# A hand-written order of steps for a delta-rule attention and a folded feed-forward: the same steps listed in another order

## The chip, the cores and the metric

One core of a Trainium2 chip runs the kernel. The metric is the device time of one execution in microseconds (us). Five engines work in parallel, each through its own instructions in the order in which they stand: TensorE (PE; its weight loads are shown as PEld), VectorE (DVE), ScalarE (ACT), GpSimd (POOL) and SyncE (SP), which here only issues DMA transfers. Engines wait for each other through semaphores.

## The reference

Two blocks, one after the other. The first is a recurrence over 768 tokens for 4 batches and 8 heads of size 48; the second is a feed-forward without a nonlinearity, in which two projections are multiplied element by element.

```python
k_n = k / (norm(k) + 1e-6)
for t in range(S):
    y[t]  = q[t] @ state
    v_old = k_n[t] @ state
    state = state + beta[t] * outer(k_n[t], v[t] - v_old)
x = y as (3072 tokens, 384)
a = x @ w1          # 384 x 1024
b = x @ w2          # 384 x 1024
h = (a * b) @ w3    # 1024 x 1024
out = h @ w_out     # 1024 x 384
```

The four weight matrices come as 64-bit floats, the rest as 32-bit floats.

## The kernel before, in words

The tokens are cut into 12 chunks of 64 per batch. Inside a chunk the recurrence is written as a triangular system: scores of keys against keys (`scores`, L357), the inverse of a unit triangular matrix (`inverse` L420 for 32 x 32 blocks of two chunks at a time, `corner` L476 for the off-diagonal blocks), and then products with the state (`chain` L543) and the outputs (`outputs` L619). The feed-forward starts from a product of weights: since no nonlinearity stands between w3 and w_out, the kernel first computes w3 @ w_out once (`fold` L756), which needs all of w_out and, transposed on TensorE, all of w3. After that each pair of chunks u (512 tokens) needs a = x @ w1, b = x @ w2, their product, and one product with the folded weights; that last one is done with seven half-size products instead of eight (`slab_sums` L835, `o` L851, `result` L901).

The kernel is written as generators. Each step has a name, a letter with a number, and each time its name comes up in the string `ORDER` (L39) it is resumed up to its next `yield`. What it issues goes to the ends of its engines' queues, and `in_text_order` (L159) fixes that order on every engine. So `ORDER` is the schedule, and nothing else decides it. The names:

- `beta`, `k0`..`k11`, `q0`, `q1`, `v0`..: loads of tokens. `p2`..: loads of k and q in another layout into one buffer each (`kperm`, `qperm`), `d2`..: their transposes on VectorE (L324). `K0`, `K1`, `Q0`, `Q1`: transposes of the first two chunks on TensorE (L337).
- `g0`..`g5` (`squares` L264) and `N0`..`N5` (`norms` L276): norms of k for two chunks, many small VectorE instructions, with one small product on TensorE each. `n0`..: v times the norm, on POOL.
- `s0`..`s11`: scores. `u0`..: their diagonal blocks stored to DRAM. `V0`..`V5`: the inverse of two chunks: V0.1 loads the blocks, two ScalarE copies bring V into PSUM (V0 and V1 only), 31 elimination steps of two VectorE instructions each follow (L440, L445), two ScalarE copies back (L449), one store (L453). `e0`..`e11`: loads of that result (L462, L469), then the corner with two products on TensorE (L498).
- `c0`..`c11`: the state chain (L551 and the VectorE lines after it). `y0`..: outputs of the chunk, copied into xT on ScalarE, and a few copies inside xT by DMA (L684).
- `P0`..`P35`: weight pieces (`piece` L695). Each is one load on SP (L699; four for w1 and w2), two ScalarE instructions (L707, L708), two VectorE instructions (L710, L711) and one POOL instruction (L715), which turn 64-bit floats into 32-bit ones. P0 to P7 are w_out, P8 to P23 are w3, P24 to P29 are w1, P30 to P35 are w2. w_out lies in the room of w2 until the folds are done. The raw data of all pieces go through five buffers in turn.
- `t0`..`t15`: transposes of the w3 pieces P8 to P23, four on TensorE and one ScalarE copy (L753). `f0`..`f7`: the folds; f7.0 needs the first half of w_out and t14, f7.1 the second half and t15, and f7.2 copies the result (L766).
- `b0`..`b7`: the a and b products of chunk 0, `a00`..`a07` those of chunk 1, `a10`.. to `a57` those of the later pairs (`ab` L772): .0 is x @ w1, .1 a ScalarE copy, .2 x @ w2, .3 the product on VectorE (L795), after which the bank is free.
- `T`: differences of the folded weights. `S0`..`S5`: sums of the products (POOL). `o0`..`o5`: the last products (L874). `x0`..`x5`: results and stores.

TensorE's results go to PSUM: four banks in turn (`bank` L149) and two double banks in turn (`two_banks` L146). A product that takes the bank of four products earlier waits until that one has been read. The transposed w3 pieces, the w3 pieces and the products a * b share ten buffers in turn (`slab` L692).

The loop that follows the string:

```python
def step(name):
    if name not in running:
        running[name] = parts[name]()
    next(running[name], None)

for name in ORDER.split():
    step(name)
in_text_order()
```

Of the kernel before, what the change touches and what calls it, by code (L numbers as in the profile page):

```python
# [36 lines left out]


ORDER = """  # L39
beta k0 P0 g0 P13 P10 P0 k1 P18 beta K0 P0 P0 P12 P13 P13 q0 P10 P18 P10 P10 K0 K0 P13 K0 beta  # L40
K0 g0 g0 q1 P8 P1 P18 g0 P12 P18 P12 K1 g0 k2 K1 K1 K1 g0 g0 P12 Q0 K1 Q0 Q0 g0 Q0 g0 P5 g0 N0
Q0 Q1 P8 P8 s0 t5 Q1 Q1 g1 Q1 Q1 s1 g1 s0 P8 g1 P9 s0 s1 s1 s1 s0 t4 t2 s0 p2 P1 P5 s0 s0 s1 s1
V0 P11 P5 P5 N0 P3 t5 P1 P1 d2 u0 P9 d2 u1 P11 P3 P9 P4 P11 N0 P3 t4 P4 P4 P9 P11 t3 t2 P2 P7
P2 P14 t0 P7 P3 P2 V0 V0 t10 P6 s1 P2 P14 t3 V0 P7 V0 V0 V0 P6 f1 g1 p3 P4 P7 t0 P14 P6 P6 P16
V0 V0 P15 V0 V0 V0 f2 V0 t10 P16 P16 f2 P15 f1 V0 f1 P16 P19 V0 V0 p2 t1 V0 P19 P19 V0 V0 f2 f0
P14 t6 t1 f0 f0 V0 P15 V0 P19 V0 v0 P15 t6 s1 P20 d2 V0 P17 P20 P20 t11 V0 P17 t11 d2 V0 t8 t8
P20 V0 k3 g1 g1 V0 g1 f5 P17 t7 V0 P17 V0 P22 P22 f5 V0 t7 V0 f5 v1 n0 V0 f3 V0 V0 s0 f3 P23
P26 V0 g1 f4 d3 t9 V0 t9 V0 d3 f4 P22 P22 f3 t14 P23 P23 P24 P24 P26 p3 t14 d3 f4 P23 n0 P30
P24 P24 s2 V0 p4 e0 g1 g1 t15 t12 f7 t15 f7 t12 f6 P26 P26 N1 e0 e0 s2 s2 P21 d3 e0 P30 e0 e0
s2 f7 s2 P25 e1 s2 c0 P21 e1 e1 e1 c0 n1 s3 P21 P21 N1 s3 y0 y0 P31 N1 s3 s3 s3 P25 P25 s3 n1  # L50
P31 c0 c0 P25 V1 P30 u2 t13 u3 P32 P30 V1 t13 e1 e1 c1 P31 V1 f6 f6 c1 c1 c1 y1 y0 b1 P32 P32
P32 y1 V1 V1 V1 b0 V1 P31 V1 b0 b2 V1 V1 b1 V1 V1 P27 P27 b1 V1 P27 V1 b1 b2 P29 P29 V1 b3 b3
P29 y1 b3 a03 V1 P28 V1 b3 P27 a01 a02 c1 a03 V1 a00 V1 k4 V1 P29 P28 P28 a01 a00 V1 V1 a00 P28
a02 a05 a00 V1 b5 V1 a05 b6 V1 V1 V1 V1 P35 p4 P35 b6 P33 a07 V1 V1 V1 V1 V1 V1 g2 a07 a04 b5
a04 b7 P33 k5 a06 b4 b7 v2 n2 a01 V1 P35 P33 a06 P34 a03 c1 V1 a03 V1 b2 V1 P35 P33 g2 P34 P34
P34 e2 b2 a01 c2 d4 d4 g2 p5 b4 b0 a04 d4 g2 g2 b0 g2 g2 e2 a07 a06 g2 g2 a04 d4 e2 n2 c2 a07
V2 b4 a06 e2 e2 e2 b5 c2 g2 N2 s4 c2 b4 S0 s4 s4 a02 a02 c2 c2 p5 T b5 T y2 b6 y2 d5 T b7 d5 d5
e3 e3 d5 N2 s4 s4 s4 N2 b7 e3 e3 v3 a05 T u4 a05 s5 b6 S0 s5 s5 S0 s5 s5 n3 o0 x0 e3 e3 s5 c3
n3 c3 S0 u5 S0 S0 S0 S0 o0 S0 S0 S0 S0 c3 c3 o0 V2 y3 x0 o0 V2 S0 V2 S0 V2 V2 V2 o0 V2 y3 V2 k6
x0 S0 g3 c3 g3 g3 S0 g3 V2 v4 x0 o0 V2 V2 V2 y3 V2 a10 a10 x0 x0 k7 x0 o0 V2 x0 x0 a17 V2 V2 V2  # L60
V2 x0 V2 V2 V2 a17 V2 V2 a15 V2 V2 a13 a16 V2 V2 v5 V2 a13 p6 V2 a16 V2 a15 V2 g3 V2 a13 g3 a13
p6 x0 a14 c3 a14 V2 e4 d6 a10 a17 a12 e4 e4 e4 g3 g3 c4 a17 g3 d6 a10 a14 d6 a12 n4 n4 c4 e4 g3
e4 e5 n5 a12 c4 a11 d6 N3 a14 c4 c4 n5 a11 y4 p7 p7 c4 e5 s6 a11 s6 s6 y4 a15 a12 a11 c5 e5 V3
a16 d7 d7 d7 d7 o1 c5 v6 a16 k8 g4 g4 e5 g4 p8 a15 g4 s7 s7 S1 e5 s7 S1 e5 x1 s7 s7 S1 s7 c5 o1
s6 S1 u7 c5 o1 s6 s6 u6 S1 S1 V3 S1 y5 c5 c5 V3 V3 V3 V3 V3 o1 S1 x1 k9 S1 y5 S1 y5 o1 S1 S1 x1
x1 V3 S1 S1 V3 c6 V3 S1 S1 V3 d8 o1 x1 x1 v7 a20 n6 x1 V3 a20 o1 x1 a23 V3 V3 x1 V3 x1 n7 a27
a24 d8 a26 V3 V3 V3 V3 x1 g4 V3 a23 V3 a25 V3 a27 a27 V3 a24 V3 V3 a26 a20 V3 g4 V3 p8 V3 V3 V3
V3 p9 V3 V3 a25 d8 n6 d8 g4 a20 a22 a22 a24 V3 c6 a27 a25 a24 a21 a21 e6 e6 e6 g4 e7 N3 e6 a25
N3 g4 s8 g4 N4 s8 e6 a22 s8 a26 e6 c6 c6 N4 s8 a26 s8 y6 a22 V4 p9 N4 S2 d9 e7 s8 a21 e7 y6 u8
d9 a21 e7 c6 a23 d9 p10 e7 d9 S2 c6 S2 s9 n7 a23 s9 e7 o2 s9 c7 s9 S2 s9 k10 S2 c7 x2 o2 c7 S2  # L70
S2 o2 u9 s9 V4 c7 V4 S2 y7 V4 V4 x2 V4 g5 g5 V4 p10 d10 y7 S2 x2 S2 o2 y7 V4 o2 x2 c7 V4 V4 S2
S2 V4 o2 a35 x2 x2 k11 x2 S2 V4 x2 S2 a35 v8 V4 S2 V4 V4 S2 V4 x2 n8 o2 a37 x2 V4 v9 V4 V4 V4
x2 a34 n8 V4 V4 a36 a30 V4 V4 V4 V4 V4 a37 V4 a34 a33 V4 g5 a33 a30 a32 a36 V4 V4 V4 V4 a34 a33
V4 V5 a32 e8 n9 c7 e8 a30 c8 a33 e8 e9 e8 g5 a35 a34 c8 a30 e8 g5 d10 a32 e9 g5 a32 g5 a36 e8
e9 S3 c8 a36 a35 a31 d10 d10 e9 a31 n9 c8 g5 c8 c8 g5 g5 e9 a31 s10 N5 e9 p11 s10 s10 a31 c9
a37 a37 p11 c9 y8 N5 v11 d11 S3 d11 d11 o3 v10 d11 s10 y8 s10 S3 u10 S3 s11 N5 s11 o3 s10 c9
s11 c9 s11 S3 x3 S3 s11 o3 S3 S3 y9 o3 s11 x3 S3 o3 u11 V5 S3 S3 V5 y9 V5 x3 n11 S3 x3 V5 V5 V5
S3 y9 S3 S3 V5 c9 V5 o3 x3 V5 x3 x3 V5 V5 x3 S3 a47 o3 x3 V5 V5 a47 x3 V5 V5 a47 n10 V5 a46 a40
a40 V5 a47 V5 a43 V5 a46 x3 a42 a45 V5 a42 V5 a41 a45 a43 V5 V5 V5 V5 V5 V5 a44 V5 a44 V5 a45
a41 V5 V5 V5 V5 c9 a42 e10 a40 e10 n11 a42 e10 a44 e10 c10 a45 n10 e11 e10 e11 c10 a43 e10 c10  # L80
c10 a40 e11 a41 a46 e11 c10 a44 S4 a43 e11 a41 S4 c10 o4 e11 a46 c11 x4 S4 S4 y10 o4 c11 c11 S4
y10 S4 S4 S4 S4 S4 c11 o4 y11 o4 x4 S4 S4 S4 o4 y11 x4 x4 o4 S4 x4 x4 S4 y11 S4 x4 x4 a50 x4 o4
a50 x4 a55 a56 a55 a52 a55 a50 a52 a56 a54 a57 a54 a55 a54 a50 a54 a51 a52 a57 a51 a53 x4 a52
a53 a51 a56 a56 a53 a51 a53 a57 o5 S5 a57 S5 S5 o5 S5 S5 S5 x5 S5 S5 S5 o5 o5 x5 S5 S5 S5 o5 S5
S5 S5 o5 x5 S5 x5 o5 x5 x5 x5 x5 x5 x5 x5 x5 x5 x5
"""


# [956 lines left out]
```

## Time and profile before

| what | value |
|---|---|
| time, median of 3 runs | 609.24 us (608.55 to 610.59) |
| profiled execution, first to last instruction | 607.4 us |
| mean granted TensorE clock | 0.966 |
| instructions | 19078 |
| PE busy | 550.0 us |
| DVE busy | 364.9 us |
| POOL busy | 177.2 us |
| ACT busy | 158.9 us |
| HBM read, written | 43.88 MB, 11.01 MB |

The profiled execution is one execution, seen from its first to its last instruction, 607.4 us; what a run needs before and after that is not in it. The page splits it into 40 slices of 15.2 us, and gives for each slice the busy share of every engine in tenths, the clock that TensorE was granted and the share of the DMA engines. Other views give the busy time of each engine in any stretch, the instructions of an engine in order of time, and whose work ended a wait. In a line such as `90.69 0.58 ACT L753 COPY w3T<-ps_f ... [5.13 <-PE ps_f L750]` the first number is the start, the second the length, then engine, line, operation and what it writes from what; in brackets stands how long the engine had been idle and what ended that.

### The profile page before, as it was taken

Reading aid. Unit: us, or ns where it says so; the run is one execution under the profiler, and the core shown is the slowest. Engines: PE = TensorE matmul, PEld = TensorE weight load, DVE = VectorE, ACT = ScalarE, POOL = GpSimd, SP = SyncE. Lnnn points to the kernel's source line nnn. Section 1 sums busy time; section 2 is a strip of 40 time slices with the busy share of each in tenths; the row PEclk is TensorE's granted clock in tenths of the full one; section 3 lists DMA queues with packets and bytes.
Section 4 is the critical chain, followed back from the end, with each engine's and each line's share of the span. In section 5 each row is a group of like instructions: output and inputs, shape, how many; then the busy total and the mean of one; then the engine's idle time right before and its main releaser. Section 6 shows DMA issues by size and latency. Waiting matters only on the chain.

```text
span 607.4 us, 19078 instructions
## 1 busy us (share of the span) xinstructions
PE 550.0 (91%) x8188; PEld 383.1 (63%) x8188; DVE 364.9 (60%) x828; ACT 158.9 (26%) x333; POOL 177.2 (29%) x223
## 2 busy tenths in 40 slices
PE   2648789678898999999999989999999999999997
PEld 2545455657777885456964559745588545984477
DVE  3768977466998489765489463894764843311012
ACT  3645534445323111222111221121112012321100
POOL 6554443122255530304420016013053000600041
PEclk9988979669999999999999999999999999999999
DMA  9968998554956347462443534435323040010001
GB/s 192 244 155 226 186 189 173 97 133 94 165 104 88 82 92 120 92 98 39 101 101 73 81 52 87 97 70 103 58 51 84 31 85 5 5 52 13 1 0 52
DMA packets 219507, 57.31 MB, mean 94 GB/s; under 512 B 206656, under 2 KB 212800, under 8 KB 219424
## 3 DMA queue, kind: packets, MB, share of 16 engines
q1 hardware_dynamic: 215232, 55.31, 45.3%
q10 hardware_dynamic: 4192, 0.79, 0.9%
q8 instruction: 64, 1.05, 0.8%
q14 instruction: 19, 0.16, 0.1%
HBM read 43.88 MB, written 11.01 MB: 90 GB/s over the span
## 4 chain that ended last, share of the span: by engine, by line
PE 75%; DVE 8%; DMA 5%; issue 4%; ACT 3%; SPq 3%; ACTq 0%; DVEq 0%
PE ps_f L779 37%; PE ps_f L874 16%; PE ps_w L551 5%; PE ps_f L759 4%; PE ps_w L652 4%; DMA raw<-in_moe_w_dram 3%; PE ps_w L498 3%; PE ps_w L367 2%; DVE tb L440 2%; PE ps_w L373 2%; SPq L230 2%; DVE ps_w L445 2%; DMA ktok<-in_k_dram 1%; ACT xT L673 1%; PE ps_f L750 1%
## 5 line engine op out<-in xcount | busy, mean ns | idle before, releaser
L779 PE MATMUL ps_f<-xT,w2s 128*128 128x512 f32 (+1 forms) x336 | 133.7, 544 | 1.6 <-issue 1.5
L779 PE MATMUL ps_f<-xT,w1s 128*128 128x512 f32 (+1 forms) x336 | 128.7, 533 | 4.5 <-DVE ab L795 2.0
L846 POOL TENSOR_TENSOR ab<-ab 128x256 f32<-128x256 f32 x96 | 67.2, 729 | 195.0 <-DVE ab L795 171.0
L779 PEld LDWEIGHTS ps_f<-xT,w1s 128*128 128x128 f32 x336 | 63.0, 190 | 60.3 <-issue 52.0
L779 PEld LDWEIGHTS ps_f<-xT,w2s 128*128 128x128 f32 x336 | 63.2, 193 | 56.2 <-issue 52.3
L791 ACT COPY ab<-ps_f 128x512 f32<-128x512 f32 (+1 forms) x56 | 28.4, 525 | 172.7 <-PE ps_f L779 161.4
L874 PE MATMUL ps_f<-w,ab 128*128 128x192 f32 x376 | 66.5, 330 | 0.0
L874 PEld LDWEIGHTS ps_f<-w,ab 128*128 128x128 f32 x376 | 61.1, 190 | 4.4 <-issue 3.5
L795 DVE TENSOR_TENSOR ab<-ab,ps_f 128x512 f32<-128x512 f32 (+1 forms) x56 | 33.2, 605 | 49.1 <-PE ps_f L779 49.0
L440 DVE TENSOR_TENSOR tb<-Vb,Ub 128x31 f32<-128x31 f32 (+15 forms) x124 | 46.0, 371 | 15.5 <-DMA Ub<-Ud 12.1
L759 PE MATMUL ps_f<-w2s,w3T 128*128 128x384 f32 x128 | 48.4, 535 | 5.7 <-ACT w3T L753 5.0
L445 DVE TENSOR_TENSOR Vb<-Vb,tb 128x31 f32<-128x31 f32 (+15 forms) x124 | 47.2, 381 | 4.3
L874 PE MATMUL ps_f<-room,ab 128*128 128x192 f32 x272 | 47.9, 330 | 1.1 <-DVE room L905 1.1
L874 PEld LDWEIGHTS ps_f<-room,ab 128*128 128x128 f32 x272 | 44.1, 190 | 1.9 <-issue 1.5
L673 ACT COPY xT<-ps_w 48x256 f32<-48x256 f32 x96 | 30.4, 365 | 48.1 <-PE ps_w L652 47.5
L759 PEld LDWEIGHTS ps_f<-w2s,w3T 128*128 128x128 f32 x128 | 26.2, 211 | 24.2 <-ACT w3T L753 5.5
L270 POOL TENSOR_TENSOR sq<-ktok 128x384 f32<-128x384 f32 x24 | 20.9, 875 | 61.4 <-DMA ktok<-in_k_dram 30.1
L367 PE MATMUL ps_w<-KQ 48*64 48x128 f32 x384 | 31.3, 308 | 3.9 <-issue 2.0
L379 DVE TENSOR_TENSOR U<-ps_w,wt 128x512 f32<-128x512 f32 x24 | 16.6, 690 | 29.9 <-PE ps_w L373 28.6
L715 POOL TENSOR_TENSOR w<-w,raw 128x512 uint32<-128x512 uint32 x16 | 20.7, 1299 | 43.6 <-DVE w L711 18.6
L373 PE MATMUL ps_w<-KQ 48*64 48x64 f32 x768 | 32.1, 242 | 0.3 <-issue 0.3
L537 POOL TENSOR_TENSOR vtok<-vtok,n 128x384 f32<-128x384 f32 x24 | 20.1, 851 | 41.0 <-DMA vtok<-in_v_dram 26.8
(109 smaller groups left out, 676.4 us busy)
## 6 DMA issues: line engine op xcount, KB each, us to landing
raw<-in_moe_w_dram SPq DMA_DIRECT2D x16, 512.0 KB, 6.2
vtok<-in_v_dram SPq DMA_DIRECT2D x24, 192.0 KB, 4.3
raw<-in_moe_w_dram SPq DMA_DIRECT2D x24, 192.0 KB, 4.0
out_dram<-osb SPq DMA_DIRECT2D x46, 96.0 KB, 2.2
ktok<-in_k_dram SPq DMA_DIRECT2D x44, 96.0 KB, 3.9
raw<-in_moe_w_out_dram SPq DMA_DIRECT2D x8, 384.0 KB, 4.8
Ud<-U SPq DMA_DIRECT2D x48, 64.0 KB, 2.1
Ub<-Ud SPq DMA_DIRECT2D x6, 512.0 KB, 3.4
```

The source lines that it names most:

```text
L367: pe.matmul(ps[half(z), 0, n : n + 128], lhsT=x[:, 0, :], rhs=x.rearrange("p j t -> p (j t)"), start=True, stop=True,)
L373: pe.matmul(ps[half(z ^ j), 1, n + C * j : n + C * j + C], lhsT=x[:, 0, :], rhs=x[:, j, :], start=True, stop=True,)
L440: dve.tensor_tensor(out=tv, in0=V[:, 0 : s + 1, s : s + 1].to_broadcast([P, s + 1, n]), in1=U[:, s, s + 1 : BS].unsqueeze(1).to_broadcast( ...
L445: dve.tensor_tensor(out=o, in0=o, in1=tv, op=ALU.subtract)
L551: pe.matmul(out(ps, r, h, z), lhsT=lhs(r, h, z), rhs=rhs(r, h, z), start=True, stop=True,)
L673: act.copy(out=xT[f, p:NP:2, b : b + NR, cc, :].rearrange("p a r t -> p r a t"), in_=pyv[f, z, b : b + NR],)
L759: pe.matmul(ps[:, 0:DM], lhsT=w3Ts[jc, kc // 4][:, kc % 4 * P : kc % 4 * P + P], rhs=wo[:, kc], start=(kc == 0), stop=(kc == KF - 1),)
L779: pe.matmul(ps[:].rearrange("p b c t -> p b (c t)"), lhsT=w[:, m, js], rhs=x[:, m, :, c0:c1].rearrange("p b c t -> p b (c t)"), start=(m = ...
L791: act.copy(out=t, in_=ps)
L795: dve.tensor_tensor(out=t, in0=t, in1=ps, op=ALU.mult)
L846: pool.tensor_tensor(out=o_, in0=x_, in1=y_, op=op)
L874: pe.matmul(ps[b][:, b, :], lhsT=abs_[u, HF * f + i][:, t0 : t0 + P], rhs=ws_[w][:, i], start=first and i == 0 and (b == 0 or n == "F"), s ...
```

## The change

The string `ORDER` is replaced by another one with the same 1317 names, each as often as before. No function is touched. All five engines get the same instructions in a different order, from the first load to the last products; the tail (o5, x5) is as before. Some places of the new string:

- SP's first loads were beta, P0, P13, P10, k1, P18; they are P10, k1, q1, P8, beta, P18. ScalarE's own queue issues q0 ahead of k0.
- w_out's eight pieces stood among P8 to P14 and P18; in the new string P5 and P2 come early and P1, P7, P6, P0, P3, P4 follow one another after P13.
- p4's first half stood between the store of V0 and the loads of e0 on SP, and now stands behind k4. v0 stood ahead of V0's store and now stands behind it. P24 and P30 stood ahead of e0 and now stand behind u2.
- f7 stood between f4 and f6 ahead of e0's first product; f7.0 now stands between e0's two products, f7.1 behind c0's second product. f6.1 stays between c1's first and second.
- In the later pairs, the a products come in another order, the w2 product of an index often directly after its w1 product.

```diff
 ORDER = """
-beta k0 P0 g0 P13 P10 P0 k1 P18 beta K0 P0 P0 P12 P13 P13 q0 P10 P18 P10 P10 K0 K0 P13 K0 beta
-K0 g0 g0 q1 P8 P1 P18 g0 P12 P18 P12 K1 g0 k2 K1 K1 K1 g0 g0 P12 Q0 K1 Q0 Q0 g0 Q0 g0 P5 g0 N0
...
-P26 V0 g1 f4 d3 t9 V0 t9 V0 d3 f4 P22 P22 f3 t14 P23 P23 P24 P24 P26 p3 t14 d3 f4 P23 n0 P30
-P24 P24 s2 V0 p4 e0 g1 g1 t15 t12 f7 t15 f7 t12 f6 P26 P26 N1 e0 e0 s2 s2 P21 d3 e0 P30 e0 e0
-s2 f7 s2 P25 e1 s2 c0 P21 e1 e1 e1 c0 n1 s3 P21 P21 N1 s3 y0 y0 P31 N1 s3 s3 s3 P25 P25 s3 n1
...
+P10 q0 Q0 k0 K0 g0 g0 g0 g0 K0 V0 K0 Q0 Q0 K0 P10 k1 g0 g0 P10 Q0 Q0 q1 Q1 P10 g0 g0 P8 K0 P8 Q1
+Q1 Q1 P8 P8 Q1 beta P18 beta beta P5 P5 g0 g0 P5 P5 K1 K1 P18 K1 P18 P18 P2 P2 P2 P2 N0 s0 t0 K1
...
+P22 P21 g1 t12 V0 t9 t8 f4 g1 P23 P23 g1 g1 P23 t9 P22 g1 g1 N1 f4 f4 t14 t14 t15 t15 v0 n0 n0
+f6 P26 N1 e0 e0 e0 s2 s2 d3 P26 e0 d3 P21 s1 N1 d3 f7 P31 P26 e0 e0 s2 P31 e1 c0 s2 t13 s2 c0 s0
+P25 y0 y0 P25 V1 c0 P26 P31 f7 u2 d3 e1 e1 e1 c0 s3 s3 s3 s3 s3 s3 P24 P28 P31 c1 c1 P24 P24 P24
...
```

## The prediction

> **What bounds the kernel now.** I read the page's engine totals and 40 slices first, then the same figures by stretch, then who TensorE waited for, then two queues in order of time where the waits pointed. Step names (s0, V0, f7.1) are those of the section on the kernel; "f7.1" is the second resumption of f7, "P24.3" the fourth of P24, counted from .0.
>
> Parts 1 and 2 of the page:
>
> ```profile
> PE 550.0 (91%) x8188; PEld 383.1 (63%) x8188; DVE 364.9 (60%) x828; ACT 158.9 (26%) x333; POOL 177.2 (29%) x223
> ...
> PE   2648789678898999999999989999999999999997
> ...
> PEclk9988979669999999999999999999999999999999
> DMA  9968998554956347462443534435323040010001
> ```
>
> TensorE is the bound, but only from the tenth slice on. Before that it starves, its clock dips, and the DMA engines are nearly full. By stretch (columns: busy of PE, PEld, DVE, ACT, POOL, then clock, DMA share, GB/s):
>
> ```profile
> 0.00:139.00 139.00, 98.11 (x1557) 70.93 (x1561) 93.09 (x202) 65.51 (x122) 59.39 (x68) 0.86 0.81 178
> 105.00:139.00 34.00, 24.79 (x859) 20.26 (x861) 17.63 (x29) 15.21 (x30) 6.66 (x7) 0.70 0.59 130
> 139.00:232.00 93.00, 86.20 (x1492) 73.36 (x1483) 73.15 (x179) 27.59 (x66) 37.40 (x44) 0.98 0.54 103
> 232.00:604.00 372.00, 365.71 (x5156) 238.85 (x5155) 198.69 (x448) 65.84 (x145) 80.39 (x112) 1.00 0.33 61
> ```
>
> At 139 us y1 ends and the first dense product (b1) begins. Idle TensorE time is 139.0 - 98.1 = 40.9 us before that, 6.8 us up to 232, 6.3 us up to 604. So an order can win much only ahead of 139 and lose much only after it. What TensorE waited for ahead of 139 (total, times, longest):
>
> ```profile
> PE ps_f L750 <- POOL w L715: 9.3, 2, 9.0
> PE ps_f L759 <- ACT w3T L753: 5.0, 2, 4.3
> ```
>
> These are weight pieces that came late. The other delay is in the chain inversion -> corner -> state, on two in-order queues, ScalarE's and SP's:
>
> ```profile
> 84.97 0.58 ACT L449 COPY Vb<-ps_w 128x512 f32<-128x512 f32 x1 [2.03 <-DVE ps_w L445]
> 90.69 0.58 ACT L753 COPY w3T<-ps_f 128x512 f32<-128x512 f32 x1 [5.13 <-PE ps_f L750]
> 91.17 0.59 ACT L449 COPY Vb<-ps_w 128x512 f32<-128x512 f32 x1
> ```
>
> ```profile
> 91.78 0.35 SPq L453 DMA_DIRECT2D Vd<-Vb  x1
> 92.23 5.46 SPq L230 DMA_DIRECT2D kperm<-in_k_dram  x8
> 97.73 0.49 SPq L462 DMA_DIRECT2D TT<-Vd  x1
> ```
>
> V0's last elimination ends on VectorE at 84.9. Its second copy then stands on ScalarE behind t9's copy, whose transposes are behind two fold halves on TensorE: 5.13 us. Then p4's eight transfers (5.46 us) stand on SP between V0's store and e0's loads.
>
> **The change part by part.** Every step is still there, so engine work, bytes and matmuls are equal; only waits can change. The sum goes against the profiled execution, span 607.4; the median of the runs shown is 609.24, 1.8 us more (start and end of the program outside the span), so a change of the span is a change of the time.
>
> *Start up to V0's eliminations.* The raw buffers (five) still pace the pieces. In the new order VectorE has P10, P8, P5, P18, P2 ahead of N0; P2 is the eighth load on SP. Loads so far, with q0 and k0 on ScalarE's queue: 3.9 MB; at the 218 to 234 GB/s of the first 30 us P2 lands near 21, its ScalarE and VectorE steps (1.0 and 0.9) end near 25, N0 begins there as before (25.0), s0's first scaling is near 30 (30.5 before), s1's last 37.6 (38.0), u1's stores leave at 38 to 40 (40.0 to 42.0). V0's load left at 47.4, behind P7 and P14; now it is behind P0 and P3, whose buffers come free near 41: 42 to 43. VectorE must still do P3 before V0; that is near 50, against 52.7. Gain 2.7; bounds -3 and +6.
>
> *V0 on VectorE.* Between first and last elimination VectorE did 31.4 us of work in 32.2. The new order leaves P6, P20, P17 and two of g1's reductions outside and takes P4 in: 28.8 us of work, 29.5 with the same gaps. End near 79.5, gain 5.4.
>
> *From V0 to e0.* t9 no longer stands ahead of the copies; f5's result (f5.1 must end, near 77), P20, P17 and P21 do, 1.2 us each on ScalarE: the second copy ends near 82.5, against 91.8. On SP p4 has gone far back, behind k4. Behind p3's q half, P23, the store, v0 and P26, e0's loads leave near 86 (97.7). v0 now follows V0's store: n0 on POOL needs it before c0, and P21's, P26's and P31's POOL parts queue behind n0; it lands near 86, c0 is due at 100, so I cost it at nothing. If that cover goes, each us is paid at t13.
> The next thing late is the norm N1: VectorE has P20, P17, P22, P21, P23 ahead of it (5.5 us), and g1's sums need TensorE behind f4.0. From V0's end the folds run without a gap (halves of 2.74, from 51.5 on): f4.0 ends near 88, N1 (4.5) near 93, f6.0 95, e0's first product near 96, against 105.3. Gain 9.3, and this replaces the gains above, which lie beside it.
>
> *e0 to y1, with f7 spread into it.* This took 34.0 us (105.3 to 139.3), with TensorE gaps of 5.5 (1.2, 0.5, 0.9, 0.7, 0.35, 0.75, 1.2). Now f7.0 and f7.1 (2.75 each at full clock, 97.4 to 102.8 before) are inside; f6.1 was already. If no gap takes them: 39.5. If they fill the gaps and the clock holds, I get 27: e0 0.8, f7.0 2.75, e0.4, s2.3, c0, y0, c0.2 with the copies between them up to 12, f7.1, s3, c1, e1, f6.1, c1.2, y1 another 12. I take 33, the middle, as the clock was reduced in part of the nearest rows:
>
> ```profile
> 110.00:120.00 10.00, 8.11 (x267) 7.44 (x267) 4.69 (x10) 2.53 (x5) 2.07 (x2) 0.51 0.45 92
> 120.00:130.00 10.00, 6.60 (x244) 5.74 (x244) 7.92 (x11) 7.27 (x16) 3.68 (x4) 0.66 0.53 120
> ```
>
> y1 ends at 96 + 33 = 129: 10.3 us earlier. Here the clock is open. The rows show 0.51 although TensorE was busy 8.1 of 10 us and no wait listed there is over 2.1 us.
>
> [...]
>
> *b and a products of the first pair, to 232.* The same 93.6 us of TensorE groups. b0.2 now comes third, so w2's first pieces are due earlier, and P24, P28, P30, P32 now stand on SP behind u2 (they were loaded at 80 to 92 and 125). From s2's last scaling: u2 3.0, P24 1.5, P28 1.7, y0's six copies 4.6, P30 1.7, u3 1.8, P32 1.8, landing 5.9 (as P32 before), then ScalarE 1.4, VectorE 1.1, POOL 2.6: about 27, so 129 for a scaling at 102; b0.2 is due at 132. Covered by 3 us; if y1 ended at 123 that cover is gone and 3 us are paid. The other moved loads (k4 and k5 swapped, v1 to v3, p4) go where DMA share is 0.54 and below; they matter only on SP: P35, k5, P34, P33, v2, k4, p4 and v3 now stand ahead of V1's store, 24 us of issue from the end of y1's copies near 136, so through at 160, and V1's last copy is due near 164. I take 0 (2 us of bank waits against the 2.0 that TensorE waited for a product's evacuation near 150); bounds -2 and +4.
>
> *From 232 on.* Two placements are tighter. After V2's first step x0.7 comes 17.4 us of VectorE work later (16.2 before), and a12 needs the bank it frees 17.3 us after c3's second product ends: 1.2 us of stall. From s5's last matmul to e4's first TensorE has 47.5 us of work; the chain through u5, V2 and e4 took 53.5 there, but 48.1 and 47.6 in the fifth and sixth pair: 2 us. a31 behind x2.9: 1. Together 4, against single stalls of 0.9, 0.2, 1.5, 0.7 and 0.8 now: 0; bounds -2 and +8. The last stores follow o5 as before: 0.
>
> Sum: -10.3 + 0 + 0. Span 597.1, time 599.
>
> **The rivals.**
> *The chain goes slower (other side).* Between e0 and y1 the clock falls to half and stays, and f7.0, f7.1, f6.1 stand in the chain at half clock. f5.1 took 5.43 so: 16.3 for three, in place of f6.1's 4.4: 34.0 - 4.4 + 16.3 = 45.9, y1 at 141.9, 2.6 late: 612. It decides from 43.3 us in this stretch. For it: 0.51 and 0.66 in just these steps. Against: the fold halves at 82 to 105 all took 2.74.
> *The clock holds.* y1 ends at 123; b0.2 then waits 3 for w2: -13.3, time 596. For it: the clock is 1.00 later, where the same small products lie between dense ones.
> *The later stages give back more.* If V2's and V5's chains take 53.5 again, against 47.5 and 47.9 of cover: 11.6 of stall in place of my 2 and 0, at worst no gain; half of that, 605. For it: 53.5 was measured. Against: 47.6 was too.
> *Nothing that counts.* A list of the same work can land within 0.3% (1.8 us, about what can be told from no change).
>
> **How the numbers follow.** Forecast 0.47 (594 to 604), clock holds 0.13, half given back 0.12: faster 0.72. Within 0.3% 0.05. Slower 0.23. The likeliest is 599. The range runs from 591 (clock holds, start 5 better) to 613 (slower chain); the likeliest one's own is 594 to 604.
>
> **What would show it.** Right: V0's last elimination near 80, its store near 83, e0's loads near 86, e0's first product near 96, y1's end near 129, then the same slope to the end, idle TensorE under 33 us ahead of b1. Wrong: e0's product after 100; a stretch over 43 us with the clock near 0.5; idle over 10 us after 232, at a12, e4 or e10; VectorE waiting for ScalarE's piece copies inside V0.

## The result, and the profile after

The new order takes 632.11 us (median of 4, 629.81 to 635.15) against 608.89 us (605.83 to 610.59) for the old one: a ratio of 1.0396, 95% interval 1.0349 to 1.0442. I had predicted 599. The profiled execution of the new order has a span of 632.2 us against 607.4, so it loses 24.8 us, and that is the loss to be explained.

Parts 1 and 2 of the page of the new order (busy us by engine; the 40 slices, now of 15.8 us):

```profile
PE 552.8 (87%) x8188; PEld 383.2 (61%) x8188; DVE 378.8 (60%) x828; ACT 159.4 (25%) x333; POOL 177.6 (28%) x223
...
PE   2653996968998889999799899699999998899997
...
PEclk9955999869999999999999999799999999899999
DMA  9669978364966543647154164147204031010001
```

TensorE did the same work in nearly the same busy time (550.0 before). VectorE did the same 828 instructions in 378.8 us, where they took 364.9: 13.9 us more for the same instructions beside other neighbours. And late in the run, too, there are slices with lower digits for TensorE and for its clock (the 26th has 6 and 7).

The stretches of the new order that answer to those shown before: up to y1's end, from e0's first product to there, up to o0.6, and the rest.

```profile
0.00:145.00 145.00, 96.30 (x1565) 67.80 (x1566) 103.94 (x204) 66.72 (x124) 60.25 (x69) 0.84 0.78 171
109.00:145.00 36.00, 29.44 (x877) 21.24 (x878) 22.33 (x37) 16.55 (x32) 6.78 (x6) 0.76 0.56 129
145.00:239.00 94.00, 85.59 (x1471) 72.99 (x1472) 71.59 (x182) 26.52 (x64) 36.48 (x43) 1.00 0.61 105
239.00:629.00 390.00, 370.88 (x5154) 242.43 (x5152) 203.32 (x443) 66.14 (x145) 80.89 (x113) 0.99 0.31 57
```

y1 ended at 145.0 where I had 129 (old order 139.3). The middle takes 94 us as before. In the rest TensorE idles 390.0 - 370.9 = 19.1 us; it was 6.3. Its busy time there is 5.2 us longer for the same products (365.7 before), so slower products are part of the loss beside the waits.

To place the loss more finely I use points at which both orders have done the same dense products: the ends of y1, o0.6, o1.6, o2.4, o2.6, o3.6 and o4.6 on TensorE. How late each kernel of this document is there, in us against the old order's profile (one profiled execution each):

| kernel | y1 | o0.6 | o1.6 | o2.4 | o2.6 | o3.6 | o4.6 | end |
|---|---|---|---|---|---|---|---|---|
| new order | 5.7 | 6.6 | 9.6 | 10.6 | 17.4 | 18.6 | 24.7 | 24.8 |
| new_front | 3.4 | 5.2 | 4.9 | 5.4 | 4.4 | 4.4 | 4.5 | 4.4 |
| old_front | -1.3 | -0.8 | 6.4 | 8.8 | 13.4 | 15.1 | 18.7 | 18.8 |
| x2_ahead | 3.5 | 4.4 | 7.4 | 7.6 | 11.0 | 11.1 | 16.9 | 17.0 |
| spaced | 4.5 | 4.9 | 13.4 | 18.0 | 23.6 | 24.8 | 26.4 | 26.5 |
| tail_mended | 3.5 | 7.5 | 19.6 | 18.7 | 18.6 | 23.9 | 25.5 | 25.5 |
| tail_mended2 | 3.9 | 5.2 | 6.7 | 9.7 | 8.7 | 14.8 | 16.4 | 16.5 |
| n0_ahead | 2.3 | 4.7 | 9.9 | 11.0 | 15.2 | 16.4 | 19.8 | 19.9 |
| n1_alone | 0.3 | 0.4 | 4.2 | 4.7 | 12.2 | 15.7 | 20.9 | 20.9 |
| early_pieces | 2.1 | 1.8 | 9.2 | 8.7 | 14.3 | 15.4 | 21.3 | 21.3 |
| all_mended | -2.0 | -0.6 | 0.3 | 3.5 | 2.6 | 8.6 | 10.2 | 10.2 |
| before_mix | -2.7 | -4.8 | 0.8 | 1.1 | 0.1 | 0.7 | 0.8 | 0.7 |
| before_mix2 | -9.9 | -12.6 | -8.4 | -8.5 | -9.4 | -9.6 | -9.6 | -9.7 |

Two things limit what the table can show. The fronts of new_front, x2_ahead, spaced, tail_mended and tail_mended2 are the new order's step for step, and y1 stands there at 3.4 to 4.5 and not at 5.7; k0 landed at 13.1 to 14.8 us in them (14.4 in the new order's profile), and V0's eliminations began at 56.8 to 58.3 (58.1). So a difference of 1 or 2 us at y1 need not be an edit's. And tail_mended2, early_pieces, all_mended and before_mix2 ran in a group in which the old order took 605.7 us, while the old order's profile is from one near 609: against their own group's old order their last column would be some 3 us higher.

So the new order's profile loses 5.7 us ahead of y1, 0.9 up to o0.6, and 18.2 behind it, most of that at two places: 6.8 between o2.4 and o2.6, 6.1 between o3.6 and o4.6.

**The front.** Who TensorE waited for up to y1's end, the waits of interest (total, times, longest):

```profile
PE ps_f L759 <- POOL w2s L715: 10.3, 1, 10.3
...
PE ps_f L255 <- DVE wt L303: 3.3, 1, 3.3
```

The first is f1.0, waiting for w_out's pieces: P0 was done at 58.7 us, when the wait ended, and P3, which the same half of the fold needs, 1.0 later. The second is N1 ahead of e0. I had put N0's start at 25. It started at 32.0, and this is VectorE's order up to there (excerpt):

```profile
15.48 0.55 DVE L272 TENSOR_REDUCE ss<-sq 128x8 f32<-128x384 f32 x1 [15.48 <-POOL sq L270]
...
19.93 0.43 DVE L710 TENSOR_SCALAR w<-w 128x512 uint32<-128x512 uint32 x1 [1.15 <-ACT w L707]
...
30.01 1.47 DVE L710 TENSOR_SCALAR w2s<-w2s 128x384 uint32<-128x384 uint32 x1 [0.17 <-ACT w2s L707]
...
31.99 0.18 DVE L279 TENSOR_SCALAR seed<-ss 128x32 uint32<-128x32 uint32 x1
```

VectorE had no work at all until 15.48, and its first conversion (P10) ran at 19.93, though P10 had landed at 4.3: on ScalarE P10 stands behind the copies of K0, and k0 landed at 14.4 instead of 10.9, because its four loads now leave behind q0's and took ScalarE until 9.07 to issue. P2 is the conversion at 30.01, and N0 (L279) stands behind it. From there everything slid: V0's eliminations began at 58.1 (predicted 50) and ended at 88.9 (79.5). SP between V0's store and e0's loads, the queue that I had expected to be cleared, did get cleared:

```profile
90.89 0.34 SPq L453 DMA_DIRECT2D Vd<-Vb  x1
91.29 1.52 SPq L213 DMA_DIRECT2D vtok<-in_v_dram  x2
92.90 2.32 SPq L699 DMA_DIRECT2D raw<-in_moe_w_dram  x4
95.32 1.96 SPq L462 DMA_DIRECT2D TT<-Vd  x4
```

e0's loads landed at 102.2, TensorE was through with f6.0 at 105.3, but e0's product began only at 109.1: N1 was not done. Two of N1's instructions in the new order, and what POOL did beside them:

```profile
102.61 1.22 DVE L291 SCALAR_TENSOR_TENSOR nr<-nt,seed 128x32 f32<-128x32 f32 x1
...
106.76 0.19 DVE L289 TENSOR_TENSOR nt<-nt,nr 128x32 f32<-128x32 f32 x1
```

```profile
102.48 1.29 POOL L715 TENSOR_TENSOR w<-w,raw 128x512 uint32<-128x512 uint32 x1
103.74 2.49 POOL L393 TENSOR_TENSOR PT<-PT,smask 128x512 f32<-128x512 f32 x2
106.17 0.95 POOL L422 MEMSET Vb<- 128x1024 f32 x1
```

An instruction of 0.19 us took 1.22 and ended with POOL's (103.83 and 103.77), and the four of its kind next to it, beside POOL's TENSOR_TENSORs too, took 0.76 to 1.19; beside the MEMSET behind them they took 0.19 again. N1's instructions took 8.1 us together instead of 4.5, and 8.6 from the first start to the last end instead of 5.0.

**Behind o0.6.** Who TensorE waited for from 232 us on, as before:

```profile
PE ps_f L874 <- DVE room L905: 6.4, 3, 5.2
PE ps_w L652 <- issue: 5.3, 4, 1.6
PE ps_w L498 <- issue: 1.8, 1, 1.8
PE ps_w L551 <- DVE S L615: 1.5, 1, 1.5
```

The longest is o2.5, seen on TensorE and then on VectorE:

```profile
394.58 0.94 PE L551 MATMUL ps_w<-X,ktok 64*48 64x48 f32 x64
400.71 5.35 PE L874 MATMUL ps_f<-room,ab 128*128 128x192 f32 x16 [5.19 <-DVE room L905]
405.90 2.74 PE L779 MATMUL ps_f<-xT,w1s 128*128 128x512 f32 x6
```

```profile
387.97 0.80 DVE L440 TENSOR_TENSOR tb<-Vb,Ub 128x31 f32<-128x31 f32 x1 [5.53 <-DMA Ub<-Ud]
...
399.68 0.42 DVE L445 TENSOR_TENSOR Vb<-Vb,tb 128x247 f32<-128x247 f32 x1
400.01 0.55 DVE L905 TENSOR_TENSOR room<-room,ps_f 128x384 f32<-128x384 f32 x1
```

o2.5 adds into the bank that x2.3 (L905) must read first. x2.3's input was ready at 394.6, but in the new order thirteen of V4's steps stand ahead of it on VectorE, and VectorE had stood still for 5.53 us before the first of them, for V4's load. After the stall o2.5 itself took 5.35 us instead of 2.8, at a granted clock of 0.52. The lines with "issue" are gaps inside runs of small products; they come below.

### The profile page after: what moved, and what is told of

The parts are those of the page before. It is cut to its first block, busy times and chain, and to the rows that moved or that the text cites. A ratio compares the mean times of both kernels' runs of the same rounds, so it can differ in the third digit from the quotient of the medians.

```text
span 632.2 us, 19047 instructions
## 1 busy us (share of the span) xinstructions
PE 552.8 (87%) x8188; PEld 383.2 (61%) x8188; DVE 378.8 (60%) x828; ACT 159.4 (25%) x333; POOL 177.6 (28%) x223
## 4 chain that ended last, share of the span: by engine, by line
PE 66%; DVE 11%; DMA 7%; issue 6%; SPq 5%; ACT 4%; POOL 1%; ACTq 0%; DVEq 0%; POOLq 0%
PE ps_f L779 35%; PE ps_f L874 13%; PE ps_w L551 5%; PE ps_w L652 3%; PE ps_w L498 3%; SPq L230 2%; PE ps_f L759 2%; DVE tb L440 2%; DMA ktok<-in_k_dram 2%; DVE Vb L445 2%; PE ps_w L367 2%; PE ps_w L373 1%; DMA xT<-xT 1%; DMA X<-in_q_dram 1%; ACT KQ L347 1%
## 5 line engine op out<-in xcount | busy, mean ns | idle before, releaser
L779 PE MATMUL ps_f<-xT,w2s 128*128 128x512 f32 (+1 forms) x336 | 132.0, 538 | 1.4 <-POOL w2s L715 1.4
L779 PE MATMUL ps_f<-xT,w1s 128*128 128x512 f32 (+1 forms) x336 | 130.0, 535 | 3.6 <-DMA xT<-xT 2.2
L874 PEld LDWEIGHTS ps_f<-w,ab 128*128 128x128 f32 x376 | 63.0, 194 | 5.1 <-issue 4.1
L759 PE MATMUL ps_f<-w2s,w3T 128*128 128x384 f32 x128 | 51.2, 557 | 10.3 <-POOL w2s L715 10.3
L874 PE MATMUL ps_f<-room,ab 128*128 128x192 f32 x272 | 50.7, 341 | 6.4 <-DVE room L905 6.4
L440 DVE TENSOR_TENSOR tb<-Vb,Ub 128x31 f32<-128x31 f32 (+15 forms) x124 | 48.8, 394 | 9.4 <-DMA Ub<-Ud 5.8
L270 POOL TENSOR_TENSOR sq<-ktok 128x384 f32<-128x384 f32 x24 | 20.9, 877 | 111.1 <-DMA out_dram<-osb 44.8
L874 PEld LDWEIGHTS ps_f<-room,ab 128*128 128x128 f32 x272 | 46.5, 198 | 7.5 <-issue 7.1
L373 PE MATMUL ps_w<-KQ 48*64 48x64 f32 x768 | 30.6, 236 | 2.3 <-issue 2.3
L379 DVE TENSOR_TENSOR U<-ps_w,wt 128x512 f32<-128x512 f32 x24 | 16.4, 685 | 27.0 <-PE ps_w L373 26.0
L367 PE MATMUL ps_w<-KQ 48*64 48x128 f32 x384 | 29.4, 298 | 3.2 <-ACT PT L391 1.8
L537 POOL TENSOR_TENSOR vtok<-vtok,n 128x384 f32<-128x384 f32 x24 | 19.9, 839 | 39.2 <-DMA vtok<-in_v_dram 30.1
```

The lines of the kernel that those rows point to most:

```text
L367: pe.matmul(ps[half(z), 0, n : n + 128], lhsT=x[:, 0, :], rhs=x.rearrange("p j t -> p (j t)"), start=True, stop=True,)
L373: pe.matmul(ps[half(z ^ j), 1, n + C * j : n + C * j + C], lhsT=x[:, 0, :], rhs=x[:, j, :], start=True, stop=True,)
L440: dve.tensor_tensor(out=tv, in0=V[:, 0 : s + 1, s : s + 1].to_broadcast([P, s + 1, n]), in1=U[:, s, s + 1 : BS].unsqueeze(1).to_broadcast( ...
L759: pe.matmul(ps[:, 0:DM], lhsT=w3Ts[jc, kc // 4][:, kc % 4 * P : kc % 4 * P + P], rhs=wo[:, kc], start=(kc == 0), stop=(kc == KF - 1),)
L779: pe.matmul(ps[:].rearrange("p b c t -> p b (c t)"), lhsT=w[:, m, js], rhs=x[:, m, :, c0:c1].rearrange("p b c t -> p b (c t)"), start=(m = ...
L874: pe.matmul(ps[b][:, b, :], lhsT=abs_[u, HF * f + i][:, t0 : t0 + P], rhs=ws_[w][:, i], start=first and i == 0 and (b == 0 or n == "F"), s ...
```

## The experiments

Steps are written with their numbers in the diffs; the string has the names alone. The old order's own median was 609.4, 610.6 and 605.7 us in the three groups of runs, so times are compared as ratios to it; the intervals are some ±0.5%, and what is smaller is read from the table above, within its limits.

### Where the loss is: half the order each

new_front is the new string up to o0.6, then all other steps in the old string's order (k4 and k5 exchanged). old_front is the other way round.

> The new order up to o0.6, the old order behind it (k4 and k5 exchanged, so that k8 finds its buffer). In the profile of the new order o0.6 ends 6.5 us later than in the old one, and 18.3 us more are lost behind it. If the two losses are independent, this is 608.9 + 6.5 = 615.4 us (613 to 618). If the second loss is a consequence of the first (chain, loads and VectorE arrive late at 232 us and stay late), the time is near 632. If the old rest has slack to make good a late start, near 609.

Measured: 614.9 us, ratio 1.0095 (1.0054 to 1.0136).

> The old order up to o0.6, the new order behind it. Independent losses: 608.9 + 18.3 = 627 us (624 to 630), with the stall at o2.5 and the gaps inside y5, y6, y10 and e10 in the trace. If the late front causes the later stalls: near 609 to 612.

Measured: 627.7 us, ratio 1.0293 (1.0250 to 1.0337).

Both came where independent losses put them, and 0.95% and 2.93% add up to 3.88% against the whole 3.96%. The late front does not cause what is lost later, and the old rest does not make it good. In old_front the stall at o2.5 was there (3.9 us) and so were 5.0 us of gaps with no releaser but issue inside y.

### The stall at o2.5

```diff
-V4.9 V4.10 ... V4.14 o2.3 o2.4 x2.1 x2.2 x2.3 c7.4 V4.15
+V4.9 o2.3 o2.4 x2.1 x2.2 x2.3 c7.4 V4.10 ... V4.15
```

> The new order with o2.3, o2.4, x2.1 to x2.3 and c7.4 moved ahead of V4.10, so that on VectorE five elimination steps stand behind x2.3 and not ahead of it. Theory: o2.5 adds into the bank that x2.3 has to read first; in the new order x2.3 stood behind eliminations that had begun only when V4's load landed, 5.19 us of stall and then 2.5 us for o2.5 at half clock. Without it 632.1 - 7.7 = 624.4 us (623 to 627). Rival: V4 is the late thing and only moves the wait (to e8 or a31): above 630.

Measured: 629.3 us, ratio 1.0358 (1.0283 to 1.0433), span 624.5. In the profile the price between o2.4 and o2.6 fell from 6.8 to 3.4; a wait of 2.25 us appeared there, for x2.5, which still stood behind V4. The profiled execution is 7.7 us shorter, but 2.2 of them lie ahead of y1, where nothing was changed, and two of the four runs were as slow as the new order (632.4, 635.0), so the time settles nothing. In the trace the mechanism is as described, and half of its price was left in.

### Small matmuls in a row

In the new order the steps of the state chain often follow each other without a dense product between them. The three cases in the profile where TensorE stopped inside such a run and waited for nothing shown:

```profile
308.80 0.33 PE L652 MATMUL ps_w<-KQ,S 48*48 48x64 f32 x8 [1.25 <-issue]
...
526.56 0.34 PE L498 MATMUL ps_w<-T,T 33*33 33x32 f32 x17 [1.76 <-issue]
...
541.43 0.33 PE L652 MATMUL ps_w<-PT,X 64*48 64x64 f32 x7 [1.58 <-issue]
```

Counted from the last dense product these came after 184, 179 and 153 recorded small matmuls (c5.4 and y5; e10.2, c10.0 and e10.4; e11.4 and y10). Behind the last one o4.0 took 4.47 us, at a granted clock of 0.63; o4.1, at 1.00, took 2.87.

```diff
-y5.0 c5.5 o1.4
+o1.4 y5.0 c5.5
-y10.0 y10.1 o4.0
+o4.0 y10.0 y10.1
```

Likewise a17.2 goes ahead of y4.0, a25.2 of y6.0, o3.2 of s10.3 and a41.2 of N5.1.

> The new order with one dense product each moved between small ones: a17.2 ahead of y4.0, o1.4 ahead of y5.0, a25.2 ahead of y6.0, o3.2 ahead of s10.3, a41.2 ahead of N5.1, o4.0 ahead of y10.0. Theory: after some 150 to 180 small matmuls without a dense product TensorE runs out of instructions, and the gaps of 0.99, 1.25, 1.49, 0.90, 1.76 and 1.58 us there (8.0 together, no releaser shown but issue) go, with some 1.6 us of o4.0 at half clock: 632.1 - 9 = 623 us (621 to 626). Rival: the gaps belong to y itself (two kinds of products with a drain between them) and stay: within 1 us of 632.

Measured: 633.5 us, ratio 1.0388 (1.0325 to 1.0450). The gaps went: of 8.0 us 0.6 was left. The time did not. Who TensorE waited for in this run behind o0.6:

```profile
PE ps_f L873 <- DVE room L904: 4.7, 2, 3.9
PE ps_w L550 <- DVE S L614: 2.8, 1, 2.8
PE ps_w L497 <- ACT xT L672: 1.8, 1, 1.8
PE ps_w L366 <- ACT xT L672: 1.8, 1, 1.8
```

(This kernel's lines are one lower: L614 is L615.) A dense product pulled ahead takes 2.8 us in front of the state chain, and TensorE met other waits instead: c6.0 waited 2.76 us for c5.5, which stands behind seven of V3's steps on VectorE, and twice TensorE waited 1.8 us for ScalarE's copies (L672) out of the bank of y4 and of y6. Only between o3.6 and o4.6, where no such block follows, was the price of 6.1 us down to 1.6. So my theory of the gaps was right about their place and wrong about their worth: in these traces taking them away gained something only where the chain behind them was not late anyway. That TensorE ran out of instructions there, as I had put it, was my guess; no run shows what it waited for.

### Mending the three places of the tail

```diff
-c5.4 V3.12 ... V3.15 k9.0 y5.0 c5.5 ... x1.3 o1.5
+c5.4 k9.0 y5.0 c5.5 ... x1.3 V3.9 ... V3.16 o1.5
-V4.9 ... V4.14 ... x2.3 c7.4 V4.15 V4.16 ... x2.4 x2.5
+x2.3 c7.4 V4.9 ... V4.12 ... x2.4 x2.5 V4.13 ... V4.16
-y10.0 y10.1 o4.0
+o4.0 y10.0 y10.1
```

And a41.2 goes ahead of N5.1, as in spaced.

> The new order with three mends behind 232 us: V3.9 to V3.16 moved behind c5.5 and x1.3; V4.9 to V4.12 behind x2.3 and V4.13 to V4.16 behind x2.5; a41.2 ahead of N5.1 and o4.0 ahead of y10.0. Theory: the new order puts an inversion's eliminations on VectorE in blocks, and what TensorE needs next (c5.5, x2.3, x2.5) stands behind the block. Gains from the profile of the new order: 1.8 us at c6.0 and o1.5, 7.7 at o2.5, and at e10 and y10, where only the gap inside a run of small matmuls is in the way, 4.5 (what the spaced run won between e10.2 and o4.6). 632.1 - 14 = 618 us (615 to 621). Rival: VectorE has too little time in these stages, and what is moved back makes the next inversion late: over 626.

Measured: 631.7 us, ratio 1.0353 (1.0291 to 1.0414): no gain to be told. In its trace:

```profile
PE ps_f L874 <- DVE osb L905: 6.3, 1, 6.3
...
PE ps_f L779 <- DVE osb L905: 3.6, 2, 2.3
```

Both are my own: the V3 steps now stood ahead of x1.5, for which o1.6 waits, and V4's ahead of x2.7 and x2.9. The places aimed at were mended (o2.4 to o2.6: -0.1 instead of 6.8; o3.6 to o4.6: 1.6 instead of 6.1). The second attempt puts V3.14 to V3.18 behind x1.5, x2.7 directly behind x2.5, V4.15 to V4.20 behind x2.9.

> As tail_mended with the mend's own faults taken out: V3.9 to V3.13 behind c5.5 and V3.14 to V3.18 behind x1.5 (in tail_mended eight steps stood ahead of x1.5, and TensorE waited 6.31 us at o1.6), V4.9 to V4.12 behind x2.3, x2.7 directly behind x2.5, V4.15 to V4.20 behind x2.9 (waits of 1.29 and 2.32 us there). Theory: the losses behind 232 us are these places: 1.8 at o1.5, 7.7 at o2.5, 4.5 at e10 to o4: 618 us (615 to 621). Rival: VectorE's work as a whole is late in these stages and every mend is paid at the next place: over 626.

Measured: 626.2 us, ratio 1.0359 (1.0303 to 1.0416), span 623.9. In time the rival is right: 626.2 lies in its range, in a group with a quick old order, and the ratio can't be told from the new order's. In the trace the three places gained what was expected: 1.5 up to o1.6 (3.0 to 1.5), 7.8 at o2.5 (6.8 to -1.0), 4.5 at o4.6 (6.1 to 1.6), 13.8 together. But 2.0 were paid back between o1.6 and o2.4 and 4.9 between o2.6 and o3.6, the latter in one wait:

```profile
PE ps_f L779 <- DVE ab L795: 3.9, 1, 3.9
```

That is a bank waiting for the product a31.3 on VectorE, which stands behind the eliminations that I had pushed back. In this trace half of what was mended is paid back at the next place. VectorE was busy 18.0 of the 19.3 us from o2.6's end to the end of that wait, but only 49.1 of the 85.0 us up to o3.6: it lacks time while an inversion runs, not in the stage as a whole. An order that puts a31.3 between the eliminations was not tried.

### The front: N0, N1, the first pieces

```diff
-g0.9 P5.2 P5.3 K1.0 K1.1 P18.1 K1.2 P18.2 ... P2.2 P2.3 N0.0
+g0.9 N0.0 P5.2 P5.3 K1.0 K1.1 P18.1 K1.2 P18.2 ... P2.2 P2.3
```

> The new order with N0.0 alone moved ahead of P5.2, K1.1, P18.2 and P2.2, right behind g0.9 on VectorE. Theory: in the new order N0 began at 32.0 us where I had counted on 25.0; s0's scalings, u0 on SP and the w_out pieces behind u0 on SP followed. With N0 at 26.6 f1.0 begins near 54 (58.8) and y1 ends 4 us earlier: 628 us (626 to 630). Rival: VectorE has no room there (it was busy nearly without a gap from 25 to 58 us), the pieces behind N0 come later by what the scores gain: f1.0 within 1.5 us of 58.8, time within 2 us of 632.

Measured: 628.3 us, ratio 1.0269 (1.0197 to 1.0341). N0 began at 26.6 as meant, but f1.0 at 57.8 and V0's eliminations at 56.8 instead of 58.8 and 58.1. The rival describes the trace: f1.0 moved by 1.0 us and V0 by 1.3, no more than the spread among unchanged fronts (P2, which stands behind N0 now, was converted 3.2 us later). y1 was 3.4 us earlier than in the new order's profile, but only 1.1 to 2.2 earlier than in the five other executions with its front. The time came out as the theory had it, the steps that were to bring it did not, so that is luck.

```diff
 n1.1 
+s1.7 s0.7
 ... g1.6
+P22.3 V0.37 v0.0 n0.0 n0.1
 g1.7 P23.3
+P21.3
```

> The new order with seven POOL instructions moved out of N1's way: s1.7 and s0.7 ahead of P20.3, P22.3 and n0 ahead of P23.3, P21.3 behind P23.3 (v0's load directly behind V0's store, as it was). Theory: N1's small instructions took 0.19 us alone and 0.76 to 1.22 us each beside POOL's; N1 took 8.1 us in the new order and 4.5 in the old one, and TensorE waited 3.3 us for it ahead of e0. With POOL idle N1 takes 4 to 5, e0.2 begins 3 us earlier, near 106, and the time is 629 us (627 to 631). Rival: the slowness is not POOL's: N1 stays at 8 us, time within 1 us of 632.

Measured: 630.3 us, ratio 1.0323 (1.0257 to 1.0390). N1 in this run:

```profile
99.91 2.02 DVE L279 TENSOR_SCALAR seed<-ss 128x32 uint32<-128x32 uint32 x1
101.97 0.19 DVE L286 SCALAR_TENSOR_TENSOR nt<-ss,seed 128x32 f32<-128x32 f32 x1
102.20 0.19 DVE L289 TENSOR_TENSOR nt<-nt,seed 128x32 f32<-128x32 f32 x1
```

```profile
100.96 0.94 POOL L422 MEMSET Vb<- 128x1024 f32 x1
```

N1 took 5.3 us from start to end (8.6 in the new order). Only its first instruction met POOL (it took 2.02 and ended with POOL's memset); those behind it took 0.19, but for the reciprocal's 0.35, which it takes in the new order too. This shows the cause of N1's slowness. e0's product no longer waited for N1 but followed f6.0, which ended at 107.1, and f7.0 behind it took 2.85 us instead of 5.49. y1 ended 5.4 us earlier than in the new order's profile, 3 to 4 earlier than in the five others with its front; the time moved by less than its interval.

```diff
-P10.0 q0.0 ... k0.0 K0.0 g0.0 ... P10.1 ... P10.2 ... P10.3
+P10.0 P0.0 P1.0 q0.0 ... k0.0 K0.0 P10.1 P0.1 P1.1 P10.2 P0.2 P1.2 P10.3 P0.3 P1.3 g0.0
```

> The new order with P0 and P1 loaded directly behind P10 and P10, P0, P1 converted ahead of the first norms and transposes. Theory: the front is late because VectorE does its first conversion at 19.9 us (8.1 in the old order) and then has 33 us of work with hardly a gap ahead of V0: three conversions of 1.1 to 1.6 us each go into the time in which it had nothing, V0.4 begins near 54 (58.1) and f1.0 near 55 (58.8), y1 ends 3 to 4 us earlier, 628.5 us (626.5 to 630.5). Rival: 0.8 MB more ahead of k0 and q1 make the first norms late by what the conversions gain: f1.0 within 1 us of 58.8, within 1.5 us of 632.

Measured: 628.6 us, ratio 1.0373 (1.0324 to 1.0422). P10 was converted at 11.6 instead of 19.9, and TensorE's wait for w_out fell from 10.3 to 5.3 us, the rest being for P3. But V0's eliminations began at 56.5 (54 expected), next to the 56.8 to 58.3 of unchanged fronts, and y1 ended 3.6 us earlier than in the new order's profile, 1.4 to 2.5 earlier than in the five others. So the folds came earlier as the theory has it, and V0 hardly did. The ratio can't tell it from no change.

### All mends together

> The new order with early_pieces, n0_ahead, n1_alone and tail_mended2 together. If the places found account for the loss, their gains add: 632 - 3.5 (early pieces) - 3 (N0) - 3 (N1) - 14 (the tail) = 608.5 us (604 to 613), near the old order. If they only hide each other (N0, N1 and the pieces all end at the same folds, the mends of the tail at the same inversions), 616 to 622.

Measured: 619.6 us, ratio 1.0226 (1.0183 to 1.0269), clear of the new order's 1.0349 to 1.0442. In its profile the front is mended: V0's eliminations began at 54.8, earlier than in any other kernel with the new front, N1 took 5.3 us, and y1 ended 2.0 us earlier than in the old order's profile. Of the tail's 18.2 us 10.8 are left, 9.2 of them in the two stages in which tail_mended2 paid back. The profile has 14.6 of 24.8 us back, some 3 of which are this group's; by the ratios it is 1.7 of the 3.96%, some 10 us. The time is in the range that I gave for gains that hide each other (616 to 622). So mending the places found brought back less than half of the loss in time; what the rest is made of stays open.

### What of the change is good: on the old order

before_mix puts onto the old order what my prediction had priced at 9.3 us.

```diff
-V0.35 t9.1 V0.36
+V0.35 V0.36 t9.1
-V0.37 p4.0 e0.0 ... f7.0 t15.1 f7.1 t12.1 f6.0 P26.2 P26.3 N1.0 e0.1 e0.2 ... e1.0
+V0.37 e0.0 ... t15.1 t12.1 f6.0 N1.0 P24.2 P24.3 P26.2 P26.3 e0.1 e0.2 f7.0 ... e1.0 p4.0 ... c0.2 f7.1 ... e1.5 f7.2
```

> The old order with those parts of the change that my prediction priced at 9.3 us, and f7 in the chain: t9.1 behind V0's second copy, p4 behind e1's loads on SP, P24 and P26 behind N1 on VectorE, f7.0 behind e0.2, f7.1 behind c0.2, f7.2 behind e1.5. The prediction's steps: e0's loads leave near 86, e0.2 at 96 to 98, y1 33 us later at 129 to 131, time 599 to 601. Theory now: e0.2 was held by TensorE's own folds and by N1, which stand there anyway. e0.2 at 100 to 102, 36 us with f7 inside (35.9 measured in the new order), y1 at 137: 607 us (605 to 609.5).

Measured: 608.6 us against 610.6, ratio 0.9955 (0.9923 to 0.9987). y1 ended at 136.6 (137 expected), but e0.2 began at 104.3, only 1.0 us earlier, not at 96 to 98 as predicted nor at 100 to 102: in the trace the gain was made behind it, where f7 went into the gaps. The second copy ended 4.1 us earlier, but the store stood behind p3 and P30 on SP, and e0.1 behind P24 and P26 on VectorE. So for e0.2 clearing two queues gained only as much as the third allowed. before_mix2 clears those as well.

```diff
-p3.1 ... P30.0 ... V0.37 e0.0
+V0.37 p3.1 ... e0.0 P30.0
-N1.0 P24.2 P24.3 P26.2 P26.3 e0.1
+N1.0 e0.1 P24.2 P24.3 P26.2 P26.3
```

> As before_mix, and three more moves of the old order ahead of e0: V0's store ahead of the second half of p3 on SP, e0's loads directly behind that half and ahead of P30, P24's and P26's VectorE steps behind e0.1. In before_mix V0's second copy ended at 87.6 us but its store left at 92.1, behind p3 and P30, and e0.1 (103.5) stood behind P24 and P26 on VectorE; TensorE was through with f6.0 at 101.7 and waited 2.57. Theory: e0.2 follows f6.0 at 101.7 to 102, y1 ends near 134 (139.3 in the old order, 136.6 in before_mix), and the rest of the old order takes a front that is 5 us earlier as it took the later one: 604.5 us against 609.5 (602.5 to 606.5). Rival: what stands behind y1 (w2's pieces, V1) comes no earlier, and TensorE waits there: 607 to 609.

Measured: 603.7 us (12 runs, 599.56 to 606.44) against 605.7 (17 runs), ratio 0.9956 (0.9927 to 0.9986). TensorE and SP in its profile:

```profile
96.75 0.76 PE L498 MATMUL ps_w<-T,U 33*33 33x32 f32 x64 [1.02 <-DVE T L481]
```

```profile
84.62 0.34 SPq L453 DMA_DIRECT2D Vd<-Vb  x1
85.06 4.63 SPq L230 DMA_DIRECT2D qperm<-in_q_dram  x8
89.73 2.08 SPq L462 DMA_DIRECT2D TT<-Vd  x4
```

The store at 84.6, e0's product at 96.8, y1's end at 129.4, f7 inside the stretch: these are the figures that I had predicted for the new order (83, 96, 129). The profiled execution is the fastest of the twelve, and the old order's profile comes from another group of runs, so the 9.7 us of the table are not the gain. The medians give 0.44%, some 2 to 3 us, just clear of no change. That is also what before_mix gained (0.9955 against 0.9956): in time the three further moves brought nothing that these runs can tell, although from V0's last elimination to e0's product the profiles show 13.3 us against 17.8 (20.4 in the old order). A little faster than the old order this kernel is, and by far faster than the new one; where the rest of the 5 us that I expected stays in the common execution is not shown.

## Why the prediction was wrong, by its own steps

- **Start up to V0's eliminations (gain 2.7; measured a loss of 5.4).** This is the step that failed first: 8.1 of the 16.0 us by which y1 missed. P2's landing was right (21.5 for 21). That its ScalarE and VectorE steps end near 25 and N0 begins there left out the queues that I had listed myself: on ScalarE the pieces stand behind K0's and Q0's copies, and these wait for k0, whose loads leave behind q0's. VectorE's first work came at 15.5 us (8.1 in the old order), its first conversion at 19.9, and from 25 us to V0 it was busy 28.8 of 33 us, with little room to catch up. What would have saved V0 is only partly shown: work given to the empty start (early_pieces) and N0 moved inside the full stretch (n0_ahead) each brought V0 1.6 and 1.3 us ahead of the new order's profile, about as much as executions of the same front differ; all_mended, which has both, brought 3.4. The lower end that I gave this term (-3) was too narrow for a start in which k0 lands 3.5 us later ahead of a busy engine.
- **V0 on VectorE (29.5 us).** 30.8. Right but for 1.3.
- **V0 to e0 (16.5 us from the last elimination to e0's product).** 20.2. The queues on ScalarE and SP were cleared as predicted: the second copy ended 1.9 us after the last elimination (6.8 in the old order), SP passed from store to loads in 4.4 us (5.9). But I had put N1 at 4.5 us, and from V0's end to N1's start 9.0; they took 8.6 and 10.9, and e0's step on VectorE behind them 0.7. For N1 n1_alone shows why: POOL's work had moved beside it.
- **e0 to y1 with f7 inside (33 us, bounds 27 and 39.5).** 35.9, inside the bounds. In before_mix2 it was 32.6. The clock was 0.76 in this stretch, and f7.0 took 5.49 us at a clock of 0.50 (a half of a fold took 2.75 at 1.00 in the old order); that is part of the difference to the better bound; the first rival, which needed 43.3 us, is out.
- **139 to 232 (0).** 0.9. Right. The SP queue was through ahead of V1's store, as predicted, but with 0.9 us to spare (177.6 us; V1's last copy ended at 178.5) where I had counted on 4.
- **From 232 on (0, bounds -2 and +8).** 18.2. The second step that failed, and the larger one. I had looked for stalls at a12, e4 and a31 and found 4 us; none of the three waited. I compared how much VectorE work stands between two steps and did not ask when the first of that work can start. The term was put at nothing without that step. At o2.5 the work could start only when V4's load had landed, so that a block of thirteen steps, at its length no worse than others, ended 5.4 us after x2.3 was due. My third rival, "the later stages give back", had the direction, with 5.8 to 11.6 us, but other places and another mechanism; and its 53.5 us are not V2's. In the old order's trace e4's first product begins 51.2 us after s5's last, and 53.4 stand between s7 and e6, in the fourth pair. That the loss lies here, whatever the front, old_front shows; for o2.5 the trace shows the step that was late, and the mends took that stall away. Of the 18.2 us the best mend still had 10.8, and of these no run shows a single cause.
- **The signs I named.** e0's product after 100 was the first sign of being wrong: 109.1. Idle over 10 us after 232 was the second: 19.1. Of the steps named only e10 stood still, for 1.8 us and with no releaser shown. A stretch over 43 us and VectorE waiting for ScalarE's copies inside V0 did not come.
- **Clock.** I had left it open and taken the middle of the two bounds. Twice it was near half just behind a long wait: o2.5 took 5.35 us at 0.52 after 5.19 us of idling, f7.0 took 5.49 us at 0.50 shortly after 3.30 us of waiting for N1. Slow products and a low clock came behind shorter waits too: in before_mix f7.0 took 3.96 us after a wait of 2.57, and the old order's clock was 0.51 at 110 to 120 us, where no wait listed is over 2.1. What sets it no run here shows.

## What to carry to other kernels

Where an order is written out for engines that work in order, as here, a step is as late as the latest start of anything ahead of it on its engine (x2.3, ready at 394.6 us, ran at 400.0, behind thirteen of V4's steps): for each product that must not wait, look at what stands ahead of its reader, and for that work's own input, above all a load. A new order of equal work is to be checked from its first microseconds on: here VectorE began 7 us later, V0 5.4 us later, and neither of two moves alone changed that clearly. And a step is held by the last of its queues, as before_mix2 against before_mix shows: of three queues, clearing two shortened the way from V0's last elimination to e0's product by 2.6 us, all three by 7.1. That an earlier step is not yet a shorter time the same pair shows, whose ratios are equal.

## What the runs showed of the hardware that I had not expected

- VectorE's small instructions with two inputs stretched to the end of POOL's TENSOR_TENSOR: in the new order's N1 0.19 us alone, 0.76 to 1.22 beside it. Beside POOL's memset (106.17 to 107.12 in the new order) they took 0.19. N1 as a whole took 8.6 us from start to end there and 5.3 in n1_alone, where POOL's work was moved away; by what POOL holds VectorE up no run shows. How much of the 13.9 us by which VectorE's 828 instructions took longer is of this kind no run separates. An instruction with a single input was hit as well (L279, 0.17 us in the old order, 1.14 in the new one beside a TENSOR_TENSOR), and in n1_alone, where it took 2.02, it ended only with the memset that followed one (at 101.93 and 101.90).
- TensorE stopped inside runs of small matmuls, each with its weight load: in the new order for 1.25, 1.76 and 1.58 us after 184, 179 and 153 recorded ones. The same run of y4 in the old sequence stopped for 0.54 us in the old order's profile and for 3.02 in before_mix's. With dense products between them (spaced) 0.6 of 8.0 us was left. The profile names issue alone as what ended these stops; their cause no run here shows.
